# A recomputed instruction order for the first 28 slices of a fused attention and ReGLU kernel, and padding copies in halves

## The chip, the cores and the metric

The kernel runs on one core of one Trainium2 chip. The metric is the time of one execution on the device in microseconds (us), as the median of several runs. TensorE (PE), VectorE (DVE), ScalarE (ACT), GpSimd (POOL) and SyncE (SP) each work through their own queue in order; a wait at the head of a queue holds all that is behind it. Transfers are asked for on the queues of SP, ACT or POOL and land later.

## The reference

The shapes are x (8, 8, 512, 64) and state (8, 8, 32, 64): batch, head, rows, head width. The attention reads in both directions, its result is laid out as 4352 rows of 512, and a gated network with d_ff = 1536 follows.

```python
scale = 1.0 / np.sqrt(D)
a = softmax(scale * x @ state.T)          # 512 x 32 per batch and head
xread = a @ state
a2 = softmax(scale * state @ x.T)         # 32 x 512
sread = a2 @ x
t = concatenate([xread, sread], axis=2)   # (B, H, 544, D)
t = t.transpose(0, 2, 1, 3).reshape(B * 544, H * D)
out = (maximum(t @ w_gate, 0) * (t @ w_val)) @ w_out
```

## The kernel before

The matmuls take bf16 inputs. For the x rows the kernel never forms `xread`. It multiplies the state of a batch into both weights first (U: `u_unit` for 512 columns of one weight at a time, `c_unit` for a range of columns of both weights while the weights still arrive; `u_out` and `c_out` copy the result from PSUM to SBUF), and then the transposed attention weights ANS into U.

Work comes in slices. A slice `gv.b.jf` is four matmuls of 128x512 for batch b and 128 of the 1536 columns: two for the gate and two for the value, in two PSUM banks. `re` (`relu`, ACT) takes the gate's bank, `mu` (`mult`, DVE) the value's bank and writes `h_sb`. There are 12 slices per batch. An output step `o.b.i` (`out_part`, line 361) is four matmuls of `h_sb` and `wo_sb`; three of them make a block of 128 output rows, which `of` (`fin_x`, line 332) copies on ACT and sends off from SP's queue.

For each batch the attention makes:

- `xT`, the transposed x: `x_T` on PE and `x_out` for batches 0 to 2, `xd` (`x_trans_dma`, line 146, a transposing transfer from SP's queue) from batch 3 on;
- scores (`sc`, PE), exponentials (`ex`, ACT), sums (`nr`, DVE) and scaled weights (`nx`, DVE), each in two halves;
- ANS, the transposed weights: `aT` and `ao` on PE and a copying engine for batches 0 and 1, `ad` (`att_aT_dma`, line 195, a transposing transfer from SP's queue) from batch 2 on;
- `sr` and `sn`, the read of the other direction. `sr_mm` needs x in SBUF with a column of ones behind each head: `xp` (`x_pad`, line 221) copies x there on POOL, into one of two buffers.

Two parts set the order. The first is written out by hand as `program` (lines 409 to 436): a list of words, taken one after the other, and each engine keeps the order in which it meets its own instructions. A word `gv.2.0@45` names a step, its arguments and the PSUM banks that it takes. `spin.n` is n matmuls on zeros that go nowhere. `dx`, `dw`, `ds` and `do` ask on POOL's queue for x, weights, state and `wo`; `stc` casts state; `on` writes the column of ones. The program covers batches 0 and 1 and slices 0 to 3 of batch 2, 28 slices in all, and output steps 0 to 9 of batch 0. The second part (lines 445 to 514) is a loop over the remaining slices with fixed places: `at(s, jf, f)` puts a step behind a slice; `at(2, 6, x_load, 4, 0, 1)` asks for x of batch 4, on POOL, behind whatever the program put there before. In this part banks come from `bank` (line 81) by turns.

Of the kernel before, what the change touches and what calls it, by code (L numbers as in the profile page):

```python
# [16 lines left out]
def kernel(  # L17
# [9 lines left out]
    nc = tc.nc  # L27

    B, H, S, D = x.shape
# [26 lines left out]
    HK = H // NK  # L56
# [12 lines left out]
    stT = const.tile([128, B, H, 64], BF16, name="stT")  # L69
# [6 lines left out]
    xf, xb, xT, e_sn, a_sn, ANS, U, hsb, sr_sb = {}, {}, {}, {}, {}, {}, {}, {}, {}  # L76
    copy = {"act": nc.scalar.copy, "dve": nc.vector.tensor_copy, "pool": nc.gpsimd.tensor_copy}

    given, turn = [], {"r": 0, "o": 1}

    def bank(name, kind="r"):

        if given:
            n = given.pop(0)
        elif kind == "spare":
            n = 6 + turn["o"] % 2
        else:
            n = turn["r"] % 6 if kind == "r" else 6 + turn["o"] % 2
            turn[kind] += 1
        return psum.tile([128, 512], FP32, name=name, tag=f"b{n}")  # L90

# [22 lines left out]
    def state_T(g):  # L114
        ps = held["st", g] = bank("stT_ps").bitcast(BF16)[:, 0:512]
        for i in range(4):
            nc.tensor.transpose(ps.rearrange("p (q i m) -> p q i m", i=4, m=8)[:, :, i],
                                st_b[:, g % 3, i].rearrange("p h d -> p (h d)"), id128)
# [31 lines left out]
    def x_T(b, lo, n):  # L150

        if b not in xT:
            xT_alloc(b)
        ps = held["xT", b, lo] = bank("xT_ps").bitcast(BF16)[:, 0:128 * n].rearrange("p (k t) -> p k t", t=128)
        for k in range(n):
            nc.tensor.transpose(ps[:, k], x_blocks(b)[:, lo + k], id128)  # L156
# [5 lines left out]
    def att_sc(b, jp):  # L162
        if b not in e_sn:
            e_sn[b] = att.tile([128, 2, NC, NJ * Ns], BF16, name="e_sn", tag="e_sn", bufs=4)
            a_sn[b] = att.tile([128, 2, NC, NJ * Ns], BF16, name="a_sn", tag="a_sn")
        t = held["sc", b, jp] = bank("sc_ps")
        ps = t.rearrange("p (r c j n) -> p r c j n", r=2, c=NC, j=2)
        for h in range(4 * jp, 4 * jp + 4):
            for k in range(2):
                nc.tensor.matmul(ps[:, h % 2, 2 * k:2 * k + 2, h // 2 % 2], xT[b][:, 2 * h + k], stT[:, b, h],  # L170
                                 start=True, stop=True)
# [49 lines left out]
    def x_pad(b):  # L221

        v = xa[:, b % NX].rearrange("p (c h) d -> p h c d", c=NC)[:, :, :, 0:D]
        nc.gpsimd.tensor_copy(out=v, in_=xb[b])  # L224

    def sr_mm(b, kind="r"):

# [170 lines left out]
    def spin(n, cols=512):  # L398
        for i in range(n):
# [6 lines left out]
             "sc": att_sc, "ex": att_exp, "nr": att_sum, "nx": att_scale, "aT2": att_T2, "ao2": att_out2, "aT": att_T, "ao": att_out,  # L406
             "c": c_unit, "co": c_out, "u": u_unit, "uo": u_out, "gv": gv, "re": relu, "mu": mult, "o": out_part,
             "of": fin_x, "xd": x_trans_dma, "ad": att_aT_dma, "xp": x_pad, "sr": sr_mm, "sn": sr_norm}
    program = """
    dx.1.0.2 dx.1.1.2 stc.0.0.act stc.0.1.act xc.0.0.dve dw.0.0.128 spin.7 stT.0@4 xc.0.1.act dw.1.0.128 on xT.0.0.4@2  # L410
    sto.0.0.dve sto.0.1.act xT.0.4.4@5 xo.0.0.4.dve dw.0.128.128 xo.0.4.4.dve dw.1.128.128 spin.1 sc.0.0@3 dw.0.256.256 ex.0.0 xT.0.8.4@0
    xT.0.12.4@1 xo.0.8.4.dve dw.1.256.256 xo.0.12.4.act nr.0.0 spin.2 sc.0.1@6 dw.0.512.256 xT.1.0.8@4 ex.0.1 nx.0.0
    xo.1.0.8.act nr.0.1 dw.1.512.256 spin.2 xT.1.8.8@2 xo.1.8.8.dve sc.1.0@5 dw.0.768.256 ex.1.0 nx.0.1 dw.1.768.256
    spin.2 c.0.0.128@30 sc.1.1@1 co.0.0.128.0.act nr.1.0 aT.0.1@6 co.0.0.128.1.act dw.0.1024.256 aT.0.0@4 ex.1.1
    ao.0.0.dve ao.0.1.act dw.1.1024.256 spin.1 c.0.128.128@25 c.1.0.128@30 nr.1.1 co.0.128.128.1.act gv.0.0@14
    co.0.128.128.0.act co.1.0.128.1.act nx.1.0 re.0.0 dw.0.1280.256 c.1.128.128@65 nx.1.1 gv.0.1@20 co.1.0.128.0.act
    co.1.128.128.0.act mu.0.0 co.1.128.128.1.act aT.1.1@7 re.0.1 dw.1.1280.256 aT.1.0@1 ao.1.1.act c.0.256.256@36
    ao.1.0.dve c.1.256.256@54 mu.0.1 co.0.256.256.0.act gv.1.1@21 dx.2.0.1 co.1.256.256.0.act co.0.256.256.1.dve
    re.1.1 gv.1.0@73 co.1.256.256.1.act mu.1.1 ds re.1.0 c.1.512.256@05 c.0.512.256@62 co.1.512.256.1.dve
    co.1.512.256.0.act gv.1.2@41 co.0.512.256.1.act mu.1.0 do.0.6 co.0.512.256.0.act gv.0.3@70 re.1.2 xp.1 gv.1.5@52  # L420
    re.0.3 mu.1.2 re.1.5 mu.0.3 gv.0.4@36 mu.1.5 re.0.4 xp.0 c.1.768.256@47 c.0.768.256@15 mu.0.4 co.1.768.256.0.act
    gv.0.2@03 co.0.768.256.0.act co.1.768.256.1.dve re.0.2 gv.0.5@26 do.6.12 co.0.768.256.1.act mu.0.2 gv.1.7@41 dx.3.0.1
    re.0.5 re.1.7 mu.0.5 gv.0.7@70 mu.1.7 re.0.7 gv.1.3@53 mu.0.7 re.1.3 gv.1.4@24 mu.1.3 re.1.4 gv.1.6@61 mu.1.4
    re.1.6 c.1.1280.256@70 c.0.1280.256@53 mu.1.6 co.1.1280.256.0.act c.1.1024.256@24 stc.1.0.pool xT.2.0.8@6
    co.0.1280.256.0.act co.1.1024.256.0.dve xT.2.8.8@1 co.0.1280.256.1.act co.1.1024.256.1.dve stc.1.1.pool
    c.0.1024.256@75 xo.2.8.8.act gv.0.10@23 co.1.1280.256.1.dve stc.3.1.pool co.0.1024.256.1.dve re.0.10 gv.1.9@40
    co.0.1024.256.0.act xo.2.0.8.dve stc.2.0.pool re.1.9 gv.0.6@12 mu.0.10 stc.3.0.pool re.0.6 mu.1.9 gv.0.11@57 mu.0.6
    stc.2.1.pool re.0.11 gv.0.8@64 mu.0.11 re.0.8 stT.1@3 gv.1.10@10 mu.0.8 sto.1.0.act sto.1.1.dve re.1.10 sc.2.0@2 o.0.0@7 ex.2.0
    mu.1.10 nr.2.0 sc.2.1@5 gv.0.9@34 ex.2.1 re.0.9 nx.2.0 o.0.1 mu.0.9 gv.1.11@12 nr.2.1 xd.3 re.1.11 o.0.2 mu.1.11
    o.0.3@6 nx.2.1 ad.2 of.0.0.act u.2.0.1024@05 u.2.1.512@34 uo.2.0.1024.0.dve uo.2.0.1024.1.act sr.0@1 sr.1@2  # L430
    uo.2.1.512.1.act sn.0 u.2.0.0@50 sn.1 xp.2 xp.3 o.0.4 uo.2.0.0.0.act uo.2.0.0.1.dve uo.2.1.512.0.dve
    o.0.5 o.0.6@7 of.0.1.act u.2.1.0@12 u.2.0.512@50 uo.2.1.0.0.act uo.2.1.0.1.dve u.2.1.1024@34 o.0.7
    uo.2.1.1024.0.act uo.2.1.1024.1.dve uo.2.0.512.0.act gv.1.8@12 uo.2.0.512.1.dve re.1.8 o.0.8 mu.1.8
    o.0.9@6 of.0.2.act gv.2.0@45 re.2.0 gv.2.2@01 mu.2.0 re.2.2 gv.2.1@23 mu.2.2 re.2.1 gv.2.3@45 mu.2.1
    re.2.3 mu.2.3
    """
    for word in program.split():
        word, _, banks = word.partition("@")
# [38 lines left out]
    for b in range(3, B):  # L477
        s = b - 1
        for i, jf in enumerate((4, 5) if b == 3 else (3, 4)):
            at(s, jf, att_half, b, i)  # L480
        for part, jf in enumerate((7, 10)):
            at(s, jf, u_block, b, part)
            paired.add(NF * s + jf)
        if b + 1 < B:
            at(s, 9, x_trans_dma, b + 1)
            at(s, 9, x_pad, b + 1)
        if b + 2 < B:
            at(s, 10, x_load, b + 2, 0, 1)
# [7 lines left out]
    for g in range(first, NF * (B + 1)):  # L496
        b, jf = divmod(g, NF)
# [47 lines left out]
```

## Time and profile before

| what | value |
|---|---|
| median of 3 runs | 221.77 us (221.62 to 222.29) |
| the profiled execution | 222.66 us |
| its span | 220.9 us |
| PE busy | 214.6 us (97%), 1955 matmuls |
| DVE, ACT, POOL busy | 130.8, 123.5, 40.6 us |
| POOL's padding copies (L224) | 8, mean 1898 ns |
| granted TensorE clock | 0.999 |

The span runs from the first to the last event of the profiled execution; the 1.8 us between it and that execution's time lie outside the profile. Busy times overlap between engines. A matmul of 512 columns is listed with 380 ns because its depth counts; matmuls behind each other start 216 ns apart.

### The profile page before, as it was taken

The page shows a single profiled execution, that of the slowest core. Times are in us where ns is not written, and L with a number is a line of the kernel's source. Part 1 is how long each engine was busy: PE and PEld are TensorE (multiplying, and loading weights), DVE is VectorE, ACT ScalarE, POOL GpSimd, SP SyncE. Part 2 cuts the span into 40 slices and gives each one's busy share as a digit, 9 for nine tenths or more (in the row PEclk, how much of TensorE's full clock was granted, in tenths as well). Part 3 has the DMA queues.
Part 4 walks back from the last instruction along what each step waited for, and adds up shares of the span by engine and source line. Part 5 has one row for each costly group of instructions (what it writes and reads, how often), then busy time and mean ns, then how long its engine had stood idle before and what let it go on. Part 6 is the DMA issues. An engine that isn't in the chain of part 4 may idle for free.

```text
span 220.9 us, 4858 instructions
## 1 busy us (share of the span) xinstructions
PE 214.6 (97%) x1955; PEld 105.2 (48%) x1955; DVE 130.8 (59%) x229; ACT 123.5 (56%) x236; POOL 40.6 (18%) x51
## 2 busy tenths in 40 slices
PE   7899999999999999999999999999999999999994
PEld 2553454444544444444444444445454445666543
DVE  5796898865787567664766487648665334222100
ACT  4699887465666565555566555646654543223221
POOL 7875830080035400040003000000000000000000
PEclk9999999999999999999999999999999999999999
DMA  7999999579057993655353105501411122222132
GB/s 165 165 195 197 198 241 204 52 213 167 8 127 112 185 142 98 142 96 103 85 130 83 50 19 142 121 16 43 112 37 53 47 47 50 50 57 85 50 95 96
DMA packets 42215, 23.65 MB, mean 107 GB/s; under 512 B 22640, under 2 KB 37872, under 8 KB 42192
## 3 DMA queue, kind: packets, MB, share of 16 engines
q0 software_dynamic: 16896, 9.05, 30.4%
q1 hardware_dynamic: 24400, 13.54, 24.3%
q10 hardware_dynamic: 896, 0.75, 1.4%
q8 instruction: 15, 0.25, 0.5%
q14 instruction: 8, 0.07, 0.1%
HBM read 18.35 MB, written 8.91 MB: 123 GB/s over the span
## 4 chain that ended last, share of the span: by engine, by line
PE 89%; DMA 7%; issue 1%; DVE 1%; POOL 1%; POOLq 0%
PE o_ps L326 39%; PE gv_ps L289 36%; PE gv_ps L306 5%; PE up L262 4%; DMA wv_sb<-in_moe_w_val_dram 4%; DMA xb<-in_x_dram 3%; PE sc_ps L170 1%; PE sr_ps L232 1%; PE o_ps L355 1%; PE upc L262 1%; PE xT_ps L156 0%; POOL xb L394 0%; DVE h_sb L317 0%; DVE stT L134 0%; POOL id masks.py:199 0%
## 5 line engine op out<-in xcount | busy, mean ns | idle before, releaser
L326 PE MATMUL o_ps<-wo_sb,h_sb 128*128 128x512 bf16 x372 | 94.6, 380 | 0.0
L289 PE MATMUL gv_ps<-ans,U 128*128 128x512 bf16 x384 | 94.1, 380 | 0.0
L317 DVE TENSOR_TENSOR h_sb<-gv_ps,g_sb 128x512 bf16<-128x512 f32 x96 | 65.3, 689 | 45.2 <-ACT g_sb L313 44.1
L313 ACT ACTIVATE g_sb<-gv_ps 128x512 bf16<-128x512 f32 (+1 forms) x108 | 63.0, 586 | 44.9 <-PE gv_ps L289 33.8
L289 PEld LDWEIGHTS <-U 128*128 128x128 bf16 x384 | 36.3, 98 | 42.2 <-issue 0.4
L326 PEld LDWEIGHTS <-h_sb 128*128 128x128 bf16 x372 | 35.3, 98 | 40.8 <-issue 2.1
L224 POOL COPY xa<-xb 128x2048 bf16<-128x2048 bf16 x8 | 15.1, 1898 | 69.2 <-PE sr_ps L232 52.2
L334 ACT COPY o_sb<-o_ps 128x512 f32<-128x512 f32 x31 | 18.3, 590 | 16.8 <-PE o_ps L326 14.8
L274 DVE CAST U<-up 128x512 bf16<-128x512 f32 x36 | 22.7, 685 | 5.7 <-PE up L262 5.6
L274 ACT CAST U<-up 128x512 bf16<-128x512 f32 x36 | 18.9, 594 | 12.1 <-PE up L262 12.0
L177 ACT ACTIVATE e_sn<-sc_ps 128x512 bf16<-128x512 f32 x16 | 9.6, 599 | 10.6 <-PE sc_ps L170 10.6
L317 DVE TENSOR_TENSOR hs_sb<-gv_ps,g_sb 128x256 bf16<-128x256 f32 x12 | 5.1, 425 | 15.1 <-PE gv_ps L306 9.2
L183 DVE TENSOR_REDUCE cs<-e_sn 128x16 f32<-128x512 bf16 x16 | 10.9, 681 | 4.4 <-ACT e_sn L177 4.4
L189 DVE TENSOR_TENSOR a_sn<-e_sn,rc 128x512 bf16<-128x512 bf16 x16 | 10.9, 686 | 0.4
L262 PEld LDWEIGHTS <-stT 64*32 64x32 bf16 x560 | 6.3, 90 | 9.6 <-issue 8.3
L284 ACT CAST U<-upc 128x512 bf16<-128x512 f32 (+1 forms) x21 | 10.0, 551 | 1.1 <-PE upc L262 1.1
L170 PEld LDWEIGHTS <-xT 128*128 128x128 bf16 x128 | 5.8, 98 | 4.4 <-issue 0.9
L262 PE MATMUL up<-wg_sb,stT 64*32 64x512 bf16 (+1 forms) x168 | 7.3, 349 | 0.0
L262 PE MATMUL up<-wv_sb,stT 64*32 64x512 bf16 (+1 forms) x168 | 7.3, 349 | 0.0
L170 PE MATMUL sc_ps<-stT,xT 128*128 128x64 bf16 x128 | 6.7, 193 | 0.5 <-DVE stT L134 0.3
L306 PE MATMUL gv_ps<-br,wg_sb 128*128 128x256 bf16 x48 | 7.2, 273 | 0.0
L306 PE MATMUL gv_ps<-br,wv_sb 128*128 128x256 bf16 x48 | 7.2, 273 | 0.0
(54 smaller groups left out, 112.9 us busy)
## 6 DMA issues: line engine op xcount, KB each, us to landing
out_dram<-o_sb SPq DMA_DIRECT2D x26, 256.0 KB, 2.4
xb<-in_x_dram POOLq DMA_DIRECT2D x6, 512.0 KB, 7.1
wo_sb<-in_moe_w_out_dram POOLq DMA_DIRECT2D x2, 768.0 KB, 13.5
out_dram<-o_sb SPq DMA_DIRECT2D x11, 128.0 KB, 2.4
wg_sb<-in_moe_w_gate_dram POOLq DMA_DIRECT2D x5, 256.0 KB, 9.4
wv_sb<-in_moe_w_val_dram POOLq DMA_DIRECT2D x5, 256.0 KB, 10.0
xb<-in_x_dram POOLq DMA_DIRECT2D x3, 256.0 KB, 5.9
st_f<-in_state_dram POOLq DMA_DIRECT2D x1, 384.0 KB, 11.5
```

What stands on the lines that cost most here:

```text
L170: nc.tensor.matmul(ps[:, h % 2, 2 * k:2 * k + 2, h // 2 % 2], xT[b][:, 2 * h + k], stT[:, b, h], start=True, stop=True)
L183: nc.vector.reduce_sum(out=cs, in_=e_v, axis=AX.X)
L189: {"dve": nc.vector, "pool": nc.gpsimd}[eng].tensor_tensor(out=by_pair(a_sn[b], jp).rearrange("p r (j n) -> p r j n", n=Ns), in0=e_v, in1= ...
L224: nc.gpsimd.tensor_copy(out=v, in_=xb[b])
L262: nc.tensor.matmul(dst[parity][32 * j:32 * j + 32], stT[r:r + 64, b, 2 * j + parity, 32 * parity:32 * parity + 32], wsb[r:r + 64, j, lo:lo ...
L274: copy[eng](out=U[b][:, w, kc, lo:lo + 512], in_=held["u", b, w, lo][kc])
L289: nc.tensor.matmul(ps[w], U[b][:, w, kc, f0:f0 + 128], ANS[b][:, kc].rearrange("p c t -> p (c t)"), start=(kc == 0), stop=(kc == NK - 1))
L306: nc.tensor.matmul(ps[w][:, 0:nt], wsb[:, j, f0:f0 + 128], br[:, j].rearrange("p b n -> p (b n)"), start=(j == 0), stop=(j == NJ - 1))
L313: nc.scalar.activation(out=g_sb[:, 0:n], in_=ps[0][:, 0:n], func=AF.Relu)
L317: nc.vector.tensor_tensor(out=dst, in0=ps[1][:, 0:n], in1=held["g", b, jf][:, 0:n], op=ALU.mult)
L326: nc.tensor.matmul(held["o", b, tsub], src[:, jf, tsub * 128:(tsub + 1) * 128], wo_sb[:, jf], start=(jf == 0), stop=(jf == NF - 1))
L334: copy[eng](out=o_sb, in_=held["o", b, tsub])
```

## The change

The program of the first 28 slices is written anew. The order of the weight transfers on POOL stays; `do.6.12` comes ahead of the padding copies, `dx.3` behind some casts and the padding of batch 0. The second state transpose and the casts move, and more spins stand in the program. On SP the order of `xd.3`, `ad.2` and the outputs changes. Each padding copy is made in two halves over the heads, in the loop's part as well. The banks of the loop start in another order.

```diff
--- before.py
+++ after.py
@@ -76,7 +76,7 @@
     xf, xb, xT, e_sn, a_sn, ANS, U, hsb, sr_sb = {}, {}, {}, {}, {}, {}, {}, {}, {}
     copy = {"act": nc.scalar.copy, "dve": nc.vector.tensor_copy, "pool": nc.gpsimd.tensor_copy}
 
-    given, turn = [], {"r": 0, "o": 1}
+    given, turn = [], {"r": 0, "o": 0}
 
     def bank(name, kind="r"):
 
@@ -85,7 +85,7 @@
         elif kind == "spare":
             n = 6 + turn["o"] % 2
         else:
-            n = turn["r"] % 6 if kind == "r" else 6 + turn["o"] % 2
+            n = (3, 5, 4, 1, 0, 2)[turn["r"] % 6] if kind == "r" else 6 + turn["o"] % 2
             turn[kind] += 1
         return psum.tile([128, 512], FP32, name=name, tag=f"b{n}")
 
@@ -221,7 +221,8 @@
     def x_pad(b):
 
         v = xa[:, b % NX].rearrange("p (c h) d -> p h c d", c=NC)[:, :, :, 0:D]
-        nc.gpsimd.tensor_copy(out=v, in_=xb[b])
+        for hs in (slice(0, HK), slice(HK, H)):
+            nc.gpsimd.tensor_copy(out=v[:, hs], in_=xb[b][:, hs])
 
     def sr_mm(b, kind="r"):
 
@@ -407,32 +408,32 @@
              "c": c_unit, "co": c_out, "u": u_unit, "uo": u_out, "gv": gv, "re": relu, "mu": mult, "o": out_part,
              "of": fin_x, "xd": x_trans_dma, "ad": att_aT_dma, "xp": x_pad, "sr": sr_mm, "sn": sr_norm}
     program = """
-    dx.1.0.2 dx.1.1.2 stc.0.0.act stc.0.1.act xc.0.0.dve dw.0.0.128 spin.7 stT.0@4 xc.0.1.act dw.1.0.128 on xT.0.0.4@2
-    sto.0.0.dve sto.0.1.act xT.0.4.4@5 xo.0.0.4.dve dw.0.128.128 xo.0.4.4.dve dw.1.128.128 spin.1 sc.0.0@3 dw.0.256.256 ex.0.0 xT.0.8.4@0
-    xT.0.12.4@1 xo.0.8.4.dve dw.1.256.256 xo.0.12.4.act nr.0.0 spin.2 sc.0.1@6 dw.0.512.256 xT.1.0.8@4 ex.0.1 nx.0.0
-    xo.1.0.8.act nr.0.1 dw.1.512.256 spin.2 xT.1.8.8@2 xo.1.8.8.dve sc.1.0@5 dw.0.768.256 ex.1.0 nx.0.1 dw.1.768.256
-    spin.2 c.0.0.128@30 sc.1.1@1 co.0.0.128.0.act nr.1.0 aT.0.1@6 co.0.0.128.1.act dw.0.1024.256 aT.0.0@4 ex.1.1
-    ao.0.0.dve ao.0.1.act dw.1.1024.256 spin.1 c.0.128.128@25 c.1.0.128@30 nr.1.1 co.0.128.128.1.act gv.0.0@14
-    co.0.128.128.0.act co.1.0.128.1.act nx.1.0 re.0.0 dw.0.1280.256 c.1.128.128@65 nx.1.1 gv.0.1@20 co.1.0.128.0.act
-    co.1.128.128.0.act mu.0.0 co.1.128.128.1.act aT.1.1@7 re.0.1 dw.1.1280.256 aT.1.0@1 ao.1.1.act c.0.256.256@36
-    ao.1.0.dve c.1.256.256@54 mu.0.1 co.0.256.256.0.act gv.1.1@21 dx.2.0.1 co.1.256.256.0.act co.0.256.256.1.dve
-    re.1.1 gv.1.0@73 co.1.256.256.1.act mu.1.1 ds re.1.0 c.1.512.256@05 c.0.512.256@62 co.1.512.256.1.dve
-    co.1.512.256.0.act gv.1.2@41 co.0.512.256.1.act mu.1.0 do.0.6 co.0.512.256.0.act gv.0.3@70 re.1.2 xp.1 gv.1.5@52
-    re.0.3 mu.1.2 re.1.5 mu.0.3 gv.0.4@36 mu.1.5 re.0.4 xp.0 c.1.768.256@47 c.0.768.256@15 mu.0.4 co.1.768.256.0.act
-    gv.0.2@03 co.0.768.256.0.act co.1.768.256.1.dve re.0.2 gv.0.5@26 do.6.12 co.0.768.256.1.act mu.0.2 gv.1.7@41 dx.3.0.1
-    re.0.5 re.1.7 mu.0.5 gv.0.7@70 mu.1.7 re.0.7 gv.1.3@53 mu.0.7 re.1.3 gv.1.4@24 mu.1.3 re.1.4 gv.1.6@61 mu.1.4
-    re.1.6 c.1.1280.256@70 c.0.1280.256@53 mu.1.6 co.1.1280.256.0.act c.1.1024.256@24 stc.1.0.pool xT.2.0.8@6
-    co.0.1280.256.0.act co.1.1024.256.0.dve xT.2.8.8@1 co.0.1280.256.1.act co.1.1024.256.1.dve stc.1.1.pool
-    c.0.1024.256@75 xo.2.8.8.act gv.0.10@23 co.1.1280.256.1.dve stc.3.1.pool co.0.1024.256.1.dve re.0.10 gv.1.9@40
-    co.0.1024.256.0.act xo.2.0.8.dve stc.2.0.pool re.1.9 gv.0.6@12 mu.0.10 stc.3.0.pool re.0.6 mu.1.9 gv.0.11@57 mu.0.6
-    stc.2.1.pool re.0.11 gv.0.8@64 mu.0.11 re.0.8 stT.1@3 gv.1.10@10 mu.0.8 sto.1.0.act sto.1.1.dve re.1.10 sc.2.0@2 o.0.0@7 ex.2.0
-    mu.1.10 nr.2.0 sc.2.1@5 gv.0.9@34 ex.2.1 re.0.9 nx.2.0 o.0.1 mu.0.9 gv.1.11@12 nr.2.1 xd.3 re.1.11 o.0.2 mu.1.11
-    o.0.3@6 nx.2.1 ad.2 of.0.0.act u.2.0.1024@05 u.2.1.512@34 uo.2.0.1024.0.dve uo.2.0.1024.1.act sr.0@1 sr.1@2
-    uo.2.1.512.1.act sn.0 u.2.0.0@50 sn.1 xp.2 xp.3 o.0.4 uo.2.0.0.0.act uo.2.0.0.1.dve uo.2.1.512.0.dve
-    o.0.5 o.0.6@7 of.0.1.act u.2.1.0@12 u.2.0.512@50 uo.2.1.0.0.act uo.2.1.0.1.dve u.2.1.1024@34 o.0.7
-    uo.2.1.1024.0.act uo.2.1.1024.1.dve uo.2.0.512.0.act gv.1.8@12 uo.2.0.512.1.dve re.1.8 o.0.8 mu.1.8
-    o.0.9@6 of.0.2.act gv.2.0@45 re.2.0 gv.2.2@01 mu.2.0 re.2.2 gv.2.1@23 mu.2.2 re.2.1 gv.2.3@45 mu.2.1
-    re.2.3 mu.2.3
+    stc.0.0.act dx.1.0.2 stc.0.1.act dx.1.1.2 dw.0.0.128 dw.1.0.128 dw.0.128.128 dw.1.128.128 dw.0.256.256
+    dw.1.256.256 dw.0.512.256 dw.1.512.256 dw.0.768.256 dw.1.768.256 dw.0.1024.256 on dw.1.1024.256 dw.0.1280.256
+    dw.1.1280.256 dx.2.0.1 ds do.0.6 do.6.12 xp.1 xc.0.0.dve spin.7 stT.0@0 xT.0.0.4@1 xo.0.0.4.act sto.0.0.dve
+    stc.2.0.pool stc.1.1.pool stc.1.0.pool sto.0.1.dve xc.0.1.dve spin.2 xT.0.4.4@2 xo.0.4.4.dve spin.2 sc.0.0@3
+    xT.0.8.4@4 ex.0.0 xT.0.12.4@5 xo.0.12.4.act xo.0.8.4.dve nr.0.0 spin.3 sc.0.1@6 ex.0.1 xT.1.0.8@0 nx.0.0 xp.0
+    xo.1.0.8.act nr.0.1 spin.3 xT.1.8.8@1 stc.2.1.pool dx.3.0.1 stc.3.1.pool stc.3.0.pool nx.0.1 sc.1.0@2 spin.2
+    aT.0.0@3 aT.0.1@4 ex.1.0 xo.1.8.8.dve sc.1.1@5 ao.0.1.act c.0.0.128@60 ex.1.1 co.0.0.128.0.act ao.0.0.dve
+    nr.1.0 c.1.0.128@21 c.0.128.128@34 spin.2 c.1.128.128@56 co.0.0.128.1.act nr.1.1 co.0.128.128.1.act
+    co.1.0.128.0.act co.0.128.128.0.act nx.1.0 gv.0.0@70 co.1.0.128.1.act re.0.0 co.1.128.128.1.act nx.1.1
+    gv.0.1@42 co.1.128.128.0.dve aT.1.0@3 aT.1.1@1 c.1.256.256@76 re.0.1 ao.1.0.dve ao.1.1.dve c.0.256.256@54
+    co.0.256.256.0.act gv.1.1@31 co.0.256.256.1.dve gv.0.3@54 re.1.1 re.0.3 mu.0.0 co.1.256.256.0.dve gv.0.2@30
+    mu.0.1 mu.0.3 co.1.256.256.1.act re.0.2 gv.1.0@75 c.1.512.256@26 re.1.0 co.1.512.256.1.act c.0.512.256@34
+    co.0.512.256.1.act mu.0.2 mu.1.0 gv.1.2@70 gv.1.3@56 co.1.512.256.0.act mu.1.1 co.0.512.256.0.dve re.1.2 re.1.3
+    c.0.768.256@41 c.1.768.256@23 gv.0.5@75 co.1.768.256.1.dve co.1.768.256.0.act gv.1.7@23 mu.1.3
+    co.0.768.256.1.act re.0.5 gv.1.4@16 re.1.7 re.1.4 co.0.768.256.0.act gv.1.5@72 mu.1.2 mu.1.7 mu.0.5 gv.0.4@03
+    re.1.5 mu.1.4 re.0.4 mu.1.5 c.1.1024.256@14 mu.0.4 c.0.1280.256@57 c.0.1024.256@60 co.0.1280.256.0.act
+    co.1.1024.256.1.act gv.0.6@23 gv.1.6@54 re.0.6 re.1.6 co.0.1024.256.0.dve co.0.1280.256.1.dve gv.0.11@67 mu.0.6
+    mu.1.6 xT.2.8.8@2 xT.2.0.8@5 c.1.1280.256@34 co.1.1024.256.0.act re.0.11 mu.0.11 gv.0.7@16 co.0.1024.256.1.act
+    re.0.7 gv.0.8@07 stT.1@1 xo.2.8.8.dve xo.2.0.8.dve re.0.8 sto.1.0.act co.1.1280.256.1.dve sto.1.1.dve
+    co.1.1280.256.0.dve gv.1.9@25 re.1.9 sc.2.0@4 gv.0.10@01 re.0.10 gv.0.9@32 sc.2.1@0 ex.2.0 re.0.9 mu.0.7 ex.2.1
+    mu.0.10 o.0.0@6 gv.1.11@41 o.0.1 gv.1.10@30 nr.2.0 re.1.11 mu.0.9 mu.0.8 re.1.10 mu.1.11 mu.1.9 mu.1.10 o.0.2
+    u.2.0.1024@24 nr.2.1 u.2.0.0@71 u.2.1.512@53 of.0.0.act sr.0@0 sr.1@6 xp.2 uo.2.0.1024.1.dve uo.2.0.0.0.act
+    uo.2.0.1024.0.act o.0.3@7 gv.1.8@42 re.1.8 sn.0 nx.2.0 nx.2.1 sn.1 uo.2.1.512.0.dve uo.2.0.0.1.dve mu.1.8 xp.3
+    o.0.4 o.0.5 o.0.6@6 u.2.1.1024@04 of.0.1.act uo.2.1.1024.1.act u.2.0.512@51 u.2.1.0@27 o.0.7 uo.2.1.0.1.dve
+    uo.2.1.512.1.dve ad.2 uo.2.1.0.0.act gv.2.0@42 o.0.8 uo.2.1.1024.0.act xd.3 o.0.9@7 gv.2.2@03 of.0.2.act re.2.2
+    gv.2.1@60 uo.2.0.512.0.dve uo.2.0.512.1.dve re.2.1 mu.2.2 gv.2.3@51 re.2.3 mu.2.3 re.2.0 mu.2.1 mu.2.0
     """
     for word in program.split():
         word, _, banks = word.partition("@")
```

## The prediction, made before the changed kernel ran

> **What bounds the kernel now.** I read the page first, then the waits of PE, then the stretches round 40 to 60 us on each queue. The page's second part shows what sets the end:
>
> ```profile
> PE   7899999999999999999999999999999999999994
> ```
>
> From slice 3 on PE never falls below 90%. Only two other things on PE can be gained: idle time near the start and the filler matmuls (spins) there. PE's waits up to 100 us:
>
> ```profile
> PE warm_ps L400 <- DVE hs_sb L372: 1.2, 1, 1.2
> PE xT_ps L156 <- DMA xb<-in_x_dram: 0.6, 2, 0.3
> PE upc L262 <- DMA wv_sb<-in_moe_w_val_dram: 0.5, 1, 0.5
> ```
>
> (total us, times, longest). No wait is left after 40 us: whatever PE now waits for there is added to the time. The stretches 0 to 10 and 10 to 20 us have 7.72 and 9.54 us of PE, so 2.74 us idle, of which 1.19 come before the first matmul and stay.
>
> The change touches one place where transfers meet. The timelines of SP, ACT, POOL and PE there (start, length, line, operation; times in us):
>
> ```profile
> 41.05 3.01 SPq L148 DMA_TRANSPOSE xT<-xb  x1
> 44.10 1.31 SPq L197 DMA_TRANSPOSE ans<-a_sn  x1
> ...
> 44.64 3.73 POOL L224 COPY xa<-xb 128x2048 bf16<-128x2048 bf16 x2 [11.68 <-issue]
> 48.32 0.88 POOL L394 DMA_DIRECT2D xb<-in_x_dram  x1
> ...
> 45.06 2.76 PE L326 MATMUL o_ps<-wo_sb,h_sb 128*128 128x512 bf16 x12
> ...
> 47.00 0.59 ACT L334 COPY o_sb<-o_ps 128x512 f32<-128x512 f32 x1 [1.23 <-PE o_ps L326]
> 47.61 0.33 SPq L338 DMA_DIRECT2D out_dram<-o_sb  x1
> ```
>
> The transpose into ans (step ad.2) starts 3.5 us before the output of.0.1 on SP, and 4.2 us before POOL asks for x of batch 4 (48.32). Landing times of such transfers, from the DMA view of small windows (at 84.1, 67.3 and 95.4 us):
>
> ```profile
> ans<-a_sn SPq DMA_TRANSPOSE x1, 3.1
> ...
> xb<-in_x_dram POOLq DMA_DIRECT2D x1, 512.0 KB, 7.3
> hs_sb<-sn SPq DMA_TRANSPOSE x1, 2.3
> xT<-xb SPq DMA_TRANSPOSE x1, 8.0
> ...
> xb<-in_x_dram POOLq DMA_DIRECT2D x1, 512.0 KB, 6.5
> out_dram<-o_sb SPq DMA_DIRECT2D x1, 256.0 KB, 2.4
> hs_sb<-sn SPq DMA_TRANSPOSE x1, 5.3
> ```
>
> A transpose issued just behind a load of x takes 8.0 us (xT, at 67.86, 0.47 after the load) or 5.3 (sn, 0.11 after it), against 4.4 and 2.2 in quiet stretches: 3.6 and 3.1 us more. An output issued at 78.25, 1.6 us into a load, took 5.4 for 2.4: 3.0 more.
>
> **The start (first 20 us).** The order of the weight loads on POOL is unchanged and their landings follow one another (wv of columns 512 on at 18.95 us, the last piece of wo at 38.30), so no weight comes much earlier. The wait for wv (0.46 us idle) should go: five gv now stand between the 256-column and the 512-column c units, two before. Against that, 21 spins instead of 15: two later spins take 0.60 us with 0.38 for the last one's depth, so 0.217 each. The 8 spins behind the first 7 cost 1.74 us, the new 14 cost 3.04. PE also changes between 128-row tiles and the small tiles 45 times instead of 48; at such a change a matmul starts 0.309 us after its predecessor and not 0.216, so 0.28 us are saved. The most that can come out: 1.55 us idle at the start + 0.35 in the stretch 30 to 40 + 1.74 + 0.28 - 3.04 = 0.9 us gained. If the six spins only come on top: 1.30 - 0.28 = 1.0 us lost. I take 0.5 gained, near the upper end: 0.4 of the idle stays, the rest is filled by spins, since the first inputs still land at the same times.
>
> **ad.2 behind of.0.1.** This is the term that decides. On SP the built order is now: of.0.0, of.0.1, ad.2, xd.3; before it was xd.3, ad.2, of.0.0, of.0.1. SP works in order, so ad.2 waits for ACT's copy of the second output block, although its own input is ready near 45 us (nx.2.1 follows sr.0's end, 43.4 below, by 0.16 + 0.29 and two of 0.69 on DVE). Behind ad.2 stand xd.3 and of.0.2. Who needs it: gv.2.0, the first matmul on ANS[2], which moved forward on PE, from behind gv.1.8, o.0.8 and o.0.9 to right behind o.0.7. PE cannot pass it.
>
> - o.0.5's last matmul starts in before at 45.06 + 7 x 0.216 = 46.57 and ends 46.95; the copy starts at 47.00. In the new order gv.1.8 stands ahead of it (4 x 0.216 = 0.86) and 0.5 are gained: it starts at 46.93, ends at 47.31.
> - ACT copy 0.59, so 47.35 to 47.95; output issue on SP 0.33 plus gaps: ad.2 issues at 48.35. Quiet, it lands after 3.1: 51.45.
> - PE after o.0.5: first matmul of o.0.6 at 47.15, then 0.86 + 0.09 + 3 u units x 0.21 + 0.09 + o.0.7's 0.86, so gv.2.0's turn is at 49.69. **Stall with a quiet transfer: 51.49 - 49.69 = 1.8 us.**
> - But it is not quiet. POOL's copies x_pad(2) and (3) begin when sr.0 is done. sr.0 now stands behind o.0.2 rather than o.0.3 (-0.86), behind one more u unit (+0.21), and 0.5 are gained: the copies start at 44.64 - 1.15 = 43.5. A copy of 2048 elements takes 1.84 from start to start, one of 256 (state) 0.34, so a half copy 0.98: four take 3.9, and the load of x for batch 4 issues at 47.4, 0.9 us ahead of ad.2, where before it came 4.2 behind. By its own row (6.9 us) it lands at 54.3.
> - The three precedents above add 3.0 to 3.6 us. Bounds for the addition: 0 and 3.6. I take 3.0: ad.2 lands at 54.45, 0.1 after the load. **Stall 4.8 us**, all on the path, since nothing else holds PE afterwards.
>
> **The clock after such a stall.** PE has no idle stretch of this length in before except at its end:
>
> ```profile
> 217.70:220.20 2.50, 0.00 (x0) 0.00 (x0) 0.23 (x1) 0.00 (x0) 0.00 (x0) 1.00 0.32 93
> 220.30:220.90 0.60, 0.00 (x0) 0.00 (x0) 0.00 (x0) 0.00 (x0) 0.00 (x0) 0.50 0.05 14
> ```
>
> The third figure from the end is the granted clock: it fell to 0.50 about 2.6 us after the last matmul (ended 217.7). At the start the spins from 1.19 us ran at 0.43 spacing, half speed, and matmuls from about 5.2 us on at full: some 4 us of work to open. So a 4.8 us stall should halve the clock, for 0 to 4 us of work: 0 to 2.0 us lost. I take the middle, 1.0.
>
> [...]
>
> **Everything else at nothing.** The halved pads add 0.13 us each to POOL, 18% busy; PE's sr of batch 4 and later stand long behind them. If that cover were gone they would cost 0.13 per batch. The load of x for batch 3 moves behind three casts and x_pad(0) on POOL: issue near 34 instead of 25.9, landing near 41, and xd.3 is asked for at 49.7. xd.3 itself may land near 57; sc.3.0 had it waiting since 46.1 in before and comes at 57.3 there, later by the stall here, so it is covered; if not, about 1 us. wo's second part is issued sooner (x_pad no longer ahead of it), still lands near 38, and o.0.1 needs it near 39.5. The bank rotation starts with 3 and 5, freed by mu.2.2 and re.2.3 just before: nothing.
>
> **Sum.** -0.5 + 4.8 + 1.0 = +5.3 us. On the profiled execution (222.66, span 220.9): 228.0. It lies 0.9 above the median of the runs (221.77), so I forecast the median: 227.1.
>
> **Rivals.**
> 1. ad.2 lands undisturbed: stall 1.8, clock stays: +1.3, 223.1. For it: its packets may get through before the load is at speed, as the load moved only 49 GB/s from 49.9 to 51.0 in before. Against: sn, issued 0.11 behind its load, was still 3.1 late.
> 2. The start loses instead (+1.0 for -0.5), the rest as forecast: 228.6. For it: the landings are the same and spins are pure time. Against: the idle it could fill is there.
> 3. ANS[2] is there in time: no stall, only the start's gain: 221.3, or 220.9 with the full 0.9. It decides if ad.2 can issue before 49.69 - 3.14 = 46.5, that is if o.0.5 ends 1.8 us earlier than I count, or PE reaches gv.2.0 that much later. Against: both are counted from the same point of PE, so a shift of the whole start moves both; only a wait of PE between o.0.5 and gv.2.0 would help.
> Chances: forecast 0.62, rival 1 0.19, rival 2 0.10, rival 3 0.09.
>
> **Range and chances.** Low end 222.9: rival 1 with the start's full gain of 0.9 (221.77 - 0.9 + 1.8 = 222.7), a little above it, since rival 3 already lies outside. High end 229.2: addition 3.6 and clock 2.0 with 0.5 gained would be 228.7, and rival 2 reaches beyond it. About 0.3% (0.7 us) is what a measurement can tell from no change. Rival 3 splits into 0.05 faster and 0.04 same, all else is slower: 0.91.
>
> **What would show it.** In the profile after: SP's order with the ans transpose behind two outputs; ans landing about 6 us after issue (3.1 would be rival 1); one wait of PE at gv_ps for DMA ans of 4.8 us (1.8) near 50; PEclk under 9 in a slice round 55; POOL copies of 128x1024, 16 of them at about 0.98; the load of x asked for near 47.4. Wrong if PE shows no wait there, or if the wait for wv at 18 us is still there.

## The result, and the profile after

The changed kernel takes 230.7 us (median of 6 runs, 230.03 to 231.59) against 221.86 us (6 runs): 1.038 times the kernel before, 95% interval 1.035 to 1.042. That is 3.6 us above the forecast (227.1) and 1.5 above the range. Its profiled execution took 230.03 us, the lowest of its runs, with a span of 228.2; before it was 222.66, 0.8 above the median. The two traces thus differ by 7.4 us, and the medians of the runs by 8.8.

PE's busy tenths and the granted clock, from the second part of the page:

```profile
PE   7899999981999999999999999999999999999995
...
PEclk9999999996799999999999999999999999999999
```

There is a hole in the tenth slice (51.4 to 57.1 us), and the clock is low in the tenth and the eleventh. PE's waits up to 110 us name it (total us, times, longest):

```profile
PE gv_ps L290 <- DMA ans<-a_sn: 5.6, 1, 5.6
...
PE xT_ps L156 <- DVE xb L138: 0.9, 1, 0.9
PE o_ps L327 <- issue: 0.9, 5, 0.2
```

The wait for wv (0.5 us) is gone, as forecast. A wait for DVE's cast of x (0.9) is new at the start, and ANS[2] holds PE for 5.6 us. The 0.9 at o_ps are no wait: this trace has 1931 of the 1961 matmuls, and in the traces of the experiments e9 and e10 below, where none is missing, the line is not there. The timelines of SP and POOL there (start, length, line, operation):

```profile
43.45 5.33 SPq L339 DMA_DIRECT2D out_dram<-o_sb  x2
48.83 1.40 SPq L197 DMA_TRANSPOSE ans<-a_sn  x1
50.35 7.25 SPq L148 DMA_TRANSPOSE xT<-xb  x1
...
44.08 4.91 POOL L225 COPY xa<-xb 128x1024 bf16<-128x1024 bf16 x4 [9.22 <-issue]
48.94 0.88 POOL L395 DMA_DIRECT2D xb<-in_x_dram  x1
```

And the transfers issued there (KB each, us from issue to landing):

```profile
xb<-in_x_dram POOLq DMA_DIRECT2D x1, 512.0 KB, 9.6
ans<-a_sn SPq DMA_TRANSPOSE x1, 7.4
xT<-xb SPq DMA_TRANSPOSE x1, 9.8
```

ad.2 goes out right behind of.0.1, 0.11 us ahead of the load of x for batch 4, and lands 7.4 us later. Stretches of PE's work and clock (PE busy and count, PEld, DVE, ACT, POOL; the clock is third from the end):

```profile
50.00:56.30 6.30, 0.74 (x4) 0.12 (x2) 2.34 (x4) 0.90 (x2) 0.00 (x0) 0.75 1.23 141
56.30:57.00 0.70, 0.69 (x2) 0.28 (x3) 0.00 (x0) 0.00 (x0) 0.00 (x0) 0.50 2.29 68
57.00:58.00 1.00, 0.78 (x3) 0.31 (x3) 0.00 (x0) 0.00 (x0) 0.00 (x0) 0.50 0.70 81
58.00:59.00 1.00, 1.00 (x3) 0.45 (x3) 0.00 (x0) 0.00 (x0) 0.00 (x0) 0.50 1.28 217
59.00:60.00 1.00, 1.00 (x4) 0.30 (x2) 0.00 (x0) 0.06 (x1) 0.00 (x0) 0.50 0.54 119
60.00:61.00 1.00, 1.00 (x6) 0.46 (x5) 0.00 (x0) 0.53 (x1) 0.00 (x0) 1.00 0.00 0
```

In the trace the clock is at half from 53.17 to 60.00 us; PE works in the last 3.69 us of that and loses half, 1.84. gv.2.0's last predecessor starts at 50.36 and gv.2.0 at 56.31: 5.95, 5.74 more than the usual 0.216. The last matmul of all starts at 225.34 instead of 217.48, 7.86 us later: 5.74 + 1.84 and 0.28 that are left over. What follows the last matmul is 0.5 us shorter than before, so the spans differ by 7.4.

A second thing came with the order. The groups of DVE's and POOL's work between 43.9 and 49 us:

```profile
L225 POOL COPY xa<-xb 128x1024 bf16<-128x1024 bf16 x4 | 4.9, 1268 | 9.2 <-issue 9.2
L189 DVE TENSOR_TENSOR a_sn<-e_sn,rc 128x512 bf16<-128x512 bf16 x2 | 2.5, 1288 | 0.0
```

nx.2.0 and nx.2.1 take 1.29 us each on average here, 0.69 elsewhere; the four half copies 4.9 us where I had counted 3.9.

### The profile page after: what moved, and what is told of

Its sections match the earlier page's. It is cut to its first block, busy times and chain, and to the rows that moved or that the text cites. A ratio compares the mean times of both kernels' runs of the same rounds, so it can differ in the third digit from the quotient of the medians.

```text
span 228.2 us, 4841 instructions
## 1 busy us (share of the span) xinstructions
PE 214.2 (94%) x1931; PEld 106.4 (47%) x1961; DVE 134.3 (59%) x235; ACT 120.0 (53%) x230; POOL 42.7 (19%) x59
## 4 chain that ended last, share of the span: by engine, by line
PE 86%; DVE 5%; DMA 5%; issue 2%; ACT 1%
PE o_ps L327 36%; PE gv_ps L290 35%; PE gv_ps L307 5%; PE up L263 3%; DMA ans<-a_sn 3%; DVE a_sn L189 2%; PE sc_ps L170 2%; PE upc L263 2%; DMA st_f<-in_state_dram 1%; PE o_ps L356 1%; PE sr_ps L233 1%; DVE cs L183 1%; DVE U L275 1%; PE xT_ps L156 1%; DVE stT L134 1%
## 5 line engine op out<-in xcount | busy, mean ns | idle before, releaser
L327 PE MATMUL o_ps<-wo_sb,h_sb 128*128 128x512 bf16 x357 | 92.9, 382 | 2.3 <-issue 1.8
L318 DVE TENSOR_TENSOR h_sb<-gv_ps,g_sb 128x512 bf16<-128x512 f32 x96 | 64.5, 688 | 50.9 <-ACT g_sb L314 49.9
L225 POOL COPY xa<-xb 128x1024 bf16<-128x1024 bf16 x16 | 17.1, 1100 | 73.5 <-PE sr_ps L233 58.9
L275 DVE CAST U<-up 128x512 bf16<-128x512 f32 x37 | 23.2, 682 | 4.0 <-PE up L263 3.9
L275 ACT CAST U<-up 128x512 bf16<-128x512 f32 x35 | 18.4, 593 | 11.5 <-PE up L263 11.5
L189 DVE TENSOR_TENSOR a_sn<-e_sn,rc 128x512 bf16<-128x512 bf16 x16 | 12.0, 761 | 0.4
L285 ACT CAST U<-upc 128x512 bf16<-128x512 f32 (+1 forms) x19 | 8.9, 529 | 1.3 <-PE upc L263 1.3
L401 PE MATMUL warm_ps<-hs_sb 128*128 128x512 bf16 x19 | 6.8, 473 | 1.4 <-DVE hs_sb L373 1.2
```

Of the source, the lines that this page charges most:

```text
L189: {"dve": nc.vector, "pool": nc.gpsimd}[eng].tensor_tensor(out=by_pair(a_sn[b], jp).rearrange("p r (j n) -> p r j n", n=Ns), in0=e_v, in1= ...
L225: nc.gpsimd.tensor_copy(out=v[:, hs], in_=xb[b][:, hs])
L275: copy[eng](out=U[b][:, w, kc, lo:lo + 512], in_=held["u", b, w, lo][kc])
L318: nc.vector.tensor_tensor(out=dst, in0=ps[1][:, 0:n], in1=held["g", b, jf][:, 0:n], op=ALU.mult)
L327: nc.tensor.matmul(held["o", b, tsub], src[:, jf, tsub * 128:(tsub + 1) * 128], wo_sb[:, jf], start=(jf == 0), stop=(jf == NF - 1))
```

## The experiments

The time of "ad.2" is that from its issue on SP to its landing; times of kernels are medians. The experiments are e1 to e11 in the order in which they stand. Their three groups of runs (e1 to e4, e5 to e8, e9 to e11) each have their own runs of the kernel before (222.23, 222.22 and 221.81 us). The changed kernel was not run again in them, so differences of a few tenths of a microsecond from its 230.7 mean nothing.

### SP's order: ad.2 ahead of of.0.1

```diff
-    ... sn.0 nx.2.0 nx.2.1 sn.1 ... ad.2 uo.2.1.0.0.act gv.2.0@42
+    ... sn.0 nx.2.0 nx.2.1 ad.2 sn.1 ... uo.2.1.0.0.act gv.2.0@42
```

> The changed kernel with one word moved: ad.2 stands right behind nx.2.1, so that SP issues it ahead of of.0.1 instead of behind it. Theory (SP's order makes the stall, and the stall closes the clock): ad.2 issues at about 47.1, where nx.2.1 ends, 1.8 us ahead of the load of x for batch 4, lands near 50.3, so PE waits at gv.2.0 for 0 to 0.5 us instead of 5.6, and the clock stays at full speed. Gain 5.6 + 1.85, so about 223.2 us. Rival (the load of x alone is to blame: ad.2 is late whenever it is in flight with the load): it lands near 54, the wait stays above 3 us, 227 us or more.

224.0 us, 1.009 times before (1.006 to 1.012). SP's timeline and the landing in this kernel:

```profile
47.17 1.34 SPq L197 DMA_TRANSPOSE ans<-a_sn  x1
...
ans<-a_sn SPq DMA_TRANSPOSE x1, 3.2
```

ad.2 issues at 47.17 and lands in 3.2 us, although the load follows at 48.98; PE does not wait for it and the clock stays at 1.00. One word takes 6.7 us back (7.1, if each kernel is compared with its own group's kernel before). What is left shows in PE's waits of this kernel:

```profile
PE sc_ps L170 <- DMA xT<-xb: 1.3, 1, 1.3
```

xd.3, now the transpose behind the load, takes 9.7 us and sc.3.0 waits for it. In the changed kernel the longer stall had covered this.

### The load of x out of the way

```diff
+    probe = const.tile([128, 1], BF16, name="probe")
     ...
+    def load_behind_ans(b):
+        nc.gpsimd.tensor_copy(out=probe, in_=ANS[2][:, 0, 0, 0:1])
+        x_load(b, 0, 1)
-    at(2, 6, x_load, 4, 0, 1)
+    at(2, 6, load_behind_ans, 4)
```

> The changed kernel, where POOL first copies one column of ANS[2], which waits for ad.2 to land, and only then asks for x of batch 4. SP's order stays. Theory (order gives 1.8 us, the load in flight gives the rest): ad.2 lands 3.1 us after its issue at 48.8, at 51.9, PE waits 1.4 us instead of 5.6, the clock stays at full speed; 230.7 - 4.2 - 1.85 = 224.6 us. Rival (something else slows ad.2, for example xd.3 directly behind it): it still takes over 6 us, and the time stays near 230.

226.97 us, 1.021 times before (1.019 to 1.024). ad.2 takes 4.5 us, neither 3.1 nor over 6; PE waits 2.6 us. The clock fell all the same, for 3.41 us: 1.7 us that I had not expected. In the changed kernel it had been twice that, 6.83. A window, in the expectations of e4 and e9, stands here for a stretch of 3.41 us.

### PE kept busy through the wait

The word `wf.n` calls `fill(n)`.

```diff
+    def fill(n):
+        ps = bank("fill_ps")
+        for i in range(n):
+            nc.tensor.matmul(ps, warm[:, 0:128], warm, start=True, stop=True)
-    ... gv.2.0@42 o.0.8
+    ... wf.26@4 gv.2.0@42 o.0.8
```

> The changed kernel with 26 matmuls of 512 columns on zeros ahead of gv.2.0 on PE, 5.6 us at 0.216 each, in place of the wait. Theory (the clock closes because PE is idle): the wait for ANS[2] ends where it did, near 56.3, and the matmuls behind it run at full speed: 1.85 us less, 228.9 us. Rival (the low clock does not come from the idle time, or the loss behind the wait is another): 230.7 or slower.

228.24 us, 2.5 us less than the changed kernel, with ad.2 at 7.9. The clock stayed open:

```profile
56.00:60.00 4.00, 3.81 (x18) 1.77 (x19) 0.00 (x0) 1.17 (x2) 0.00 (x0) 1.00 0.83 152
```

So the low clock of this kernel (0.50 from 53.17 to 60.00 us) came from the idle time. The two profiled executions differ by 1.9 us: 1.84 gained by the clock and 0.57 at the start (first scores at 6.95 us, not 7.52; the clock had opened at 3.90 us, not 5.38, which the edit does not touch), 0.46 lost because ad.2 took longer. Why the medians differ by 2.5 is not shown.

### SP's new order alone, in the kernel before

```diff
-    ... nr.2.1 xd.3 re.1.11 ... nx.2.1 ad.2 of.0.0.act ... of.0.1.act u.2.1.0@12
+    ... nr.2.1 re.1.11 ... nx.2.1 of.0.0.act ... of.0.1.act ad.2 xd.3 u.2.1.0@12
```

> The kernel before with SP's order of the changed kernel alone: of.0.0, of.0.1, ad.2, xd.3. gv.2.0 keeps its place on PE, where its turn comes near 51.9. ad.2 would issue near 48.0, 0.3 us ahead of the load of x for batch 4. Theory (a transpose in flight with the load takes 7.4 us): it lands near 55.4, PE waits some 3.5 us, the clock closes for part of one window or not at all: 221.8 + 3.5 to + 5 = 225 to 227. Rival (ad.2 lands in 3.1 to 4 us): no wait, 221.8 us.

227.22 us (225.51 to 228.63), 1.022 times before (1.016 to 1.028). The profiled execution is the slowest of the four (228.63): ad.2 takes 8.0 us, PE waits 3.8, the clock falls for 6.83 us. In the fastest (225.51) the mean granted clock is 1.00: there it did not fall. Two words moved in the old program give 5 of the 8.8 us, although gv.2.0 stands later there.

### xd.3 back at the head of SP's order

```diff
-    ... of.0.0.act ... o.0.8 uo.2.1.1024.0.act xd.3 o.0.9@7
+    ... xd.3 of.0.0.act ... o.0.8 uo.2.1.1024.0.act o.0.9@7
```

(on top of the kernel with ad.2 moved)

> The kernel of e1_ad_early with xd.3 also moved, to the head of SP's order, ahead of of.0.0, where it stands in the kernel before. In e1 xd.3 was issued at 49.3, 0.3 us behind the load of x for batch 4, took 9.7 us, and sc.3.0 waited 1.3 us for it (1.45 between the starts beyond the usual distance). Theory (SP's order makes this wait too): xd.3 goes out when x of batch 3 lands, near 41, and the wait is gone: 224.0 - 1.4 = 222.6 us, and what is left against the kernel before is the start. Rival (the wait moves on to another step): 223.5 or more.

222.39 us, 1.0014 times before (0.9999 to 1.003). The wait at sc.3.0 is gone. With these two words moved, the new order costs nothing that these runs can tell.

### nx ahead of the padding copies

```diff
-    ... nr.2.0 re.1.11 ... sn.0 nx.2.0 nx.2.1 ad.2 sn.1
+    ... nr.2.0 nx.2.0 re.1.11 ... nx.2.1 ad.2 sn.0 sn.1
```

(on top of the last one)

> The kernel of e5_xd_early with nx.2.0 and nx.2.1 ahead of sn.0 on DVE, so that they run before or at the start of POOL's four half copies instead of among them. In the changed kernel nx.2.0 and nx.2.1 took 1.06 and 1.52 us for 0.69 and two half copies 1.50 for 1.04. Theory (DVE's two-input multiplication and POOL's copy shut each other out): nx.2.0 takes 0.69, the copies together some 4.1 us for 4.9, the load of x goes out 0.8 us sooner; PE's wait of 0.3 us at the u unit of columns 1024 to 1536 goes, so 0.3 us or less against e5. Rival (the long nx have another cause): the durations stay. On the whole time both say about the same as e5, 222.3 to 222.6.

221.97 us, 0.998 times before (0.997 to 0.9995). nx.2.0 is out of the copies' way and takes 0.69. nx.2.1 still meets the first copies and takes 1.40; one copy, the one among them, takes 1.50, the others 1.04.

### The cast of x on ACT at the start

```diff
-    ... xc.0.0.dve spin.7 ... xc.0.1.dve spin.2 xT.0.4.4@2
+    ... xc.0.0.dve xc.0.1.act spin.7 ... spin.2 xT.0.4.4@2
```

(on top of the last one)

> The kernel of e6_nx_early with the cast of the second quarter of x (xc.0.1) on ACT right behind the state's casts, where in the changed kernel it stands on DVE behind two copies of the state and ends 1.1 us later; PE waited 0.9 us for it. Theory (this wait, with spins around it, is the start's loss): the first scores start near 6.5 instead of 7.5 and 0.6 to 0.9 us are gained against e6, which makes it equal to the kernel before or faster, 221.4 to 221.8. Rival (the weights' landing sets the start, so spins and waits only change places): no gain, as e6.

221.58 us, 0.997 times before (0.996 to 0.998), and 0.4 us under e6. The kernel before with the halves alone (e8, next) has 221.67, so against an old order with the same copies nothing is gained that these runs can tell. The first scores start at 6.54 us instead of 7.37, but a wait for x of batch 1 takes half of that back:

```profile
PE xT_ps L156 <- DMA xb<-in_x_dram: 0.5, 1, 0.5
```

### The halves alone, in the kernel before

```diff
-        nc.gpsimd.tensor_copy(out=v, in_=xb[b])
+        for hs in (slice(0, HK), slice(HK, H)):
+            nc.gpsimd.tensor_copy(out=v[:, hs], in_=xb[b][:, hs])
```

> The kernel before with the padding copies in halves alone. Each pad takes 2.03 us of POOL instead of 1.90 and the load of x for batch 4 goes out 0.2 us later; nx.2.0 and nx.2.1 have run before the copies start here. Theory (the halves cost nothing by themselves): the same time within 0.3%, nx at 0.69. Rival (halves cost through POOL): slower by 0.5 us or more.

221.67 us, 0.998 times before (0.997 to 0.999): no loss, but 0.5 us less, which its trace does not explain (its last matmul starts 0.29 us later than in the trace of before). nx keeps 0.69 us, as it runs before the copies here.

### ad.2 behind of.0.1, with xd.3 out of its way

```diff
-    ... of.0.0.act ... o.0.8 uo.2.1.1024.0.act xd.3 o.0.9@7
+    ... xd.3 of.0.0.act ... o.0.8 uo.2.1.1024.0.act o.0.9@7
```

(in the changed kernel)

> The changed kernel with xd.3 at the head of SP's order and ad.2 left behind of.0.1. ad.2 is then in flight with the load of x for batch 4, but no transpose stands behind it. In the changed kernel (load and xd.3) ad.2 took 7.4 us, in e2 (xd.3 only) 4.5. Theory A, as the prediction had it (the load alone adds some 3 us): ad.2 takes 6.1, lands near 54.9, PE waits 4.3 us and the clock falls for one or two windows: 222.4 + 4.3 + 1.7 = 228.4 us. Theory B (the load matters only through xd.3): ad.2 takes 3.1 to 4.5, a wait of 1.4 to 2.8: 224 to 226.5.

229.73 us, 1.036 times before (1.032 to 1.040).

```profile
ans<-a_sn SPq DMA_TRANSPOSE x1, 6.9
```

ad.2 takes 6.9 us with the load 0.12 us behind it and no transpose beside it: theory A, 0.8 more than it said.

### ad.2 behind of.0.1, with neither beside it

(the last edit in the kernel whose load waits for ANS[2])

> The kernel of e2_load_late (POOL asks for x of batch 4 only when ANS[2] has landed) with xd.3 at the head of SP's order too, so that ad.2, still behind of.0.1, has neither the load nor xd.3 beside it. Theory (a quiet transpose takes 3.1 us): it lands at 51.95, PE waits 1.4 to 1.6 us, the clock stays at full speed as the idle time is under the 2.6 us that closed it: 222.4 + 1.5 = 223.9 us. Rival (the output of.0.1, issued 0.4 us ahead, slows it as well): 4 us or more, 225.

225.98 us, 1.019 times before (1.015 to 1.022). That median lies between two kinds of runs: 225.11 and 225.34 with a mean granted clock of 1.00, 226.62 and 226.76 with 0.992. The profiled one (226.62) has the clock closed for 3.41 us, and PE works in 2.9 of them: a cost of 1.45 us, which is what lies between the two kinds. So a stall of about the same length (PE's wait is 2.7 us in the profiled one) closed the clock in two executions of this kernel and, as their times and clocks say, left it alone in the other two.

```profile
ans<-a_sn SPq DMA_TRANSPOSE x1, 4.6
```

ad.2 takes 4.6 us with nothing of either beside it. My theory fell: 4.5 in e2 was not xd.3's doing. The four kernels together:

| ad.2 behind of.0.1 | load of x beside it | load later |
|---|---|---|
| xd.3 right behind | 7.4 us | 4.5 us |
| xd.3 long before | 6.9 us | 4.6 us |

So the load adds 2.3 to 2.9 us. xd.3 adds 0.5 or nothing: e3, with both beside it like the changed kernel, took 7.9 for 7.4, so 0.5 is within what two executions of this arrangement differ by. And 1.5 us over the quiet 3.1 come from something else.

The output of.0.1 is not it: in e10 ad.2's packets start 1.1 us behind its issue and go at the pace of the quiet transfer at 84.2 us in the trace of before, some 200 in 0.25 us, until 50.68 us. Then a packet of instructions (queue q8 in the views, 16 KB, 1.12 us long) starts, and what is left of ad.2 trickles in until 52.7 us. The same stands in e2 (packet at 50.78); in e1 and e5 it came at 51.0 and 50.2, after ad.2 had landed. The trace of before shows it too, in the transposes into ans and in the window of the slowest of them (62.2 to 67.1 us, no load of x beside it):

```profile
DMA to landing us min/median/max: 3.1/3.1/4.9
...
q8 instruction: 1, 0.02, 1.7%
ans<-a_sn SPq DMA_TRANSPOSE x1, 4.9
```

In all 13 traces together, 69 transposes into ans have no load of x issued beside them. Twelve take 4.5 to 5.0 us, and in each such a packet starts 1.9 to 3.1 us behind the issue; ten of them have no output issued within 2 us ahead. The other 57 take 3.0 to 3.2, and of these only three see a packet before they land, at 2.98 us or later (one of the twelve, in e11, sees it no sooner, at 3.07). No run moves the packet by itself: the traces agree, but it is not an experiment.

### Whole padding copies in the new order

```diff
-        for hs in (slice(0, HK), slice(HK, H)):
-            nc.gpsimd.tensor_copy(out=v[:, hs], in_=xb[b][:, hs])
+        nc.gpsimd.tensor_copy(out=v, in_=xb[b])
```

> The changed kernel with each padding copy in one piece again. nx.2.0 and nx.2.1 still fall among POOL's copies for batches 2 and 3. Theory (copy and two-input multiplication shut each other out, one whole instruction at a time): one of nx.2.0 and nx.2.1 takes 2 us or more, waiting for a copy of 1.9, and a copy takes up to 0.7 longer; the pair of nx together takes about as long as in halves (2.5 us) or longer. The time stays within 0.5 us of the changed kernel, 230.2 to 231.2, since ad.2 waits for of.0.1 anyway. Rival (the halves are what makes the collision, a whole copy does not): both nx at 0.69.

233.57 us, 1.053 times before (1.050 to 1.056). The two nx, by minimum, median and maximum:

```profile
L189 DVE TENSOR_TENSOR a_sn<-e_sn,rc x2: 1929/2152/2375, 44.5 to 46.3; 128x512 bf16<-128x512 bf16 x2
```

DVE is held 4.2 us instead of 2.5, so a wait of PE for sn.1 appears (1.5 us), and the load of x, now 0.6 us ahead of ad.2, brings that to 10.0 us. The mechanism was right, the time was not: in this order the halves save 2.9 us.

## Why the prediction was right or wrong

**ad.2 behind of.0.1: right.** It is the cause. Moving it ahead takes 6.7 to 7.1 of the 8.8 us back, xd.3 another 1.6, and the remaining 0.14% cannot be told from no change. SP's order alone slows the old program by 5 us. Issue and turn came at 48.83 and 50.58 instead of 48.35 and 49.69.

**The addition for the load: mis-sized, the largest miss of the sum.** I took 3.0 on top of 3.1, with 3.6 as the upper bound from three precedents. Measured were 7.44, 4.3 on top. e9 and e10 split it: the load gives 2.3, which my rows had, and 1.5 are there without the load, where I had nothing: the quiet 3.1 was no floor for this place. The packet of instructions that goes with these 1.5 us in the traces could have been seen beforehand: the slowest transpose into ans of before (4.9 us) has one in its middle, and another starts at 51.33 us in that trace, inside the flight that I forecast (48.35 to 54.45). I used the median of 3.1 and passed over the maximum. The stall came to 5.74 for 4.8.

**The clock: right in kind, mis-sized.** 1.84 us for 1.0, near the upper bound of 2.0, and e3 shows that idle PE is the cause here: with matmuls in place of the wait the clock was 1.00 from 50 to 60 us. My row (closed 2.6 us after the last matmul) was no threshold: in e9 the clock fell at 51.87, 1.8 us after PE went idle, and in two of the four runs of e10, with a wait of PE of 2.7 us, it fell as well. A wait of 1.5 us (e11) did not close it. Rival 1, and with it the low end, assumed that a stall of 1.8 us leaves the clock alone: no run shows that, and e9 makes it doubtful. The lengths at full and half speed that begin and end inside a trace are all multiples of 3.41 us: 215.04 in before, 47.79 and 6.83 in after, 3.41 in e2 and e10. In the 3.41 us that ended with the fall at 51.87 in e9 PE had still worked for 1.6.

**The start: the gain did not come.** I had 0.5 gained; the two traces leave 0.3 lost, inside my lower bound of 1.0. The sign is not shown: with the same order up to there, the first output step starts anywhere from 37.64 (e9) to 38.37 us (e6) in the traces of the new order, at 37.17 (e4) and 37.99 in those of the old. I counted idle time and spins and did not follow DVE's queue at the start: the cast of x's second quarter moved there, behind two state copies, and PE waited 0.9 us. With the cast on ACT (e7) the time falls by 0.4 us; then the new order equals the old one with halves (221.58 and 221.67). I also counted five gv between the two c units; there are four, and the wait for wv went all the same.

**The padding copies: costed at nothing, and wrong in this order.** I followed what waits for POOL and not what runs on DVE beside it. The traces show nx and the copies taking turns. In that of after nx.2.0 ends 0.54 us behind the first half copy, the second copy 0.90 behind nx.2.0, nx.2.1 0.54 behind that copy, and the third copy 0.90 behind nx.2.1; sn.0 and the casts of U beside the same copies keep their 0.29 and 0.68. The 0.69 of nx becomes 1.06 and 1.52 beside half copies and 1.93 and 2.38 beside whole ones (e11), and stays 0.69 where no copy runs (e8). In the changed kernel this costs little by itself (0.4 us between e5 and e6), but it lengthened the four copies from 3.9 us to 4.9, and that, with copies that began 0.6 us later than I had counted, put the load of x at 48.94 instead of 47.4.

**xd.3: right on the condition.** I said that the stall covers it and that it costs about 1 us otherwise; without the stall it cost 1.3 us of waiting, 1.6 in all.

**The high end.** It was a sum of two bounds with the start's gain left in. Of the 3.6 us between forecast and result, the three terms give 2.6 in the traces (stall 0.9, clock 0.8, start 0.8), all on the slow side, and the shorter end takes 0.5 of that back. The other 1.5 are no event in the kernel: the profiled execution of before lay 0.9 us above the median that I had, which I carried over, and that of after lies 0.7 below its own.

## What to carry to other kernels

When an order is recomputed, write down for every queue, those that only issue transfers included, what now stands ahead of each transfer that a matmul needs; two words on SP were worth 8 us here, more than the start could ever give. A landing time measured in a quiet place does not hold for the same transfer beside a large load (3.1 us became 7.4): take the slowest row, look in the trace for what makes it slow, a packet of instructions too, and add the clock that the wait may close. Put a DVE multiplication like nx and GpSimd's copies at different times (two nx took 2.5 us here for 1.3), or cut the copies so that each blocks the other for less (beside whole copies the two took 4.2).

## What the runs showed of the hardware that was not expected

- A transposing transfer of 1024 packets (one ANS) takes 3.0 to 3.2 us alone, and 4.5 to 5.0 where a 16 KB packet of instructions falls into it (12 of 12 in 13 traces). With such a packet and a 512 KB load from POOL's queue, issued 0.11 to 0.35 us behind it, it took 6.9 to 8.0 us (e9 6.9, after 7.4, e3 7.9, e4 8.0); with the load 0.6 us ahead, 10.0 (e11). Issued 1.8 us ahead of the load it still took 3.2 (e1). The load suffers too: 9.6 us beside two transposes (after), 6.9 in the kernel before.
- The clock halved after 1.8 us of idle PE (e9), and came back only 6.8 us later although PE worked again from 3.2 us after the fall. In e10, with a wait of PE of 2.7 us, it fell in two of four executions of one kernel.
- nx and the padding copies shut each other out, instruction by instruction: in the trace after their ends alternate, 0.54 us from a copy's to the next nx's and 0.90 back, and 0.69 becomes 1.06 and 1.52 for nx, 1.04 becomes 1.50 for two copies.
